# Top-k attention and an MLP on one core: last rows selected first, VectorE turning them, and another order of the first steps

## The chip, the core and the metric

The kernel runs on one core of a Trainium2 chip. The metric is the device time of one execution in microseconds (us); the median of three runs before the change is 1659.19 us (1656.96 to 1659.20). The profile is one execution of 1655.8 us from first to last instruction.

The core's engines run side by side and wait for each other by semaphores: TensorE (PE; its weight loads are PEld), VectorE (DVE), ScalarE (ACT), GpSimd (POOL), and SyncE (SP), which here only issues DMA transfers.

## What is computed

```python
# q, k, v: (8 batches, 8 heads, 576 rows, 64)
scores = q @ k.T / sqrt(64)
kth    = 32nd largest score of each row
scores = where(scores >= kth, scores, -1e9)
attn   = exp(scores - rowmax) / (rowsum + 1e-9)
x      = concat_heads(attn @ v)                  # (8, 576, 512)
xn     = (x - mean) / sqrt(var + 1e-6) * g_ln
out    = x + relu(xn @ w_ch1) @ w_ch2            # 512 -> 2048 -> 512
```

The 576 rows of a head are four whole tiles of 128 rows and 64 last rows. Heads are handled in pairs: a **unit** is one tile number of one head pair. For a whole tile it has two halves, t = 0 and 1, one for each head (128 x 576 scores each); for the last rows both heads share one half (64 + 64 rows).

## The kernel before

There are 160 units. They are processed in steps, one per unit: in step `n` VectorE selects unit `n`, while other engines work on its neighbours. Units belong to groups; from batch 2 on a batch has for each of its four head pairs one group with tiles 0, 1 and the last rows, and later one with tiles 2 and 3. A group is multiplied with the values together, one step after its last unit has been turned.

Selection of the 32nd largest score uses a split: the row's 576 scores are halved into pairs, the larger of each pair goes to `hi`, the smaller to `lo`. GpSimd makes `lo` in two passes, with integers:

```python
def halve(u):
    nc.vector.tensor_tensor(hi, a, b, ALU.max)                                  # L375
    nc.gpsimd.tensor_tensor(lo..I32, a..I32, hi..I32, ALU.subtract)             # L376
    nc.gpsimd.tensor_tensor(lo..I32, lo..I32, b..I32, ALU.add)                  # L379

def select(u, i):
    # i == 0: the 16 largest of lo, by MAX8 (L391) and match_replace (L386), appended to hi
    # i == 1, 2, 3: the 32 largest of hi, 8 at a time, MAX8 (L399) and match_replace (L386)
    #               i == 1 takes the first 8, i == 2 the next 8, i == 3 the last 16
```

After the selection ScalarE masks (L426) and exponentiates (L436) the scores into `e`. To be multiplied with the values, `e` must be turned (keys to partitions) into the tile `pt`, which has one buffer. There are two ways. TensorE transposes 128x128 pieces into PSUM and ScalarE copies them:

```python
def turn(u):
    def part(t):                    # 4 transposes (L490), then copies into pt
        for c in range(J):
            nc.tensor.transpose(ps[...], u.e[:, t, ...], ident[:])
        # last rows: two copies of 128x256 (L497); whole tile: one of 128x512 (L502)
    def last():                     # the keys left over at the end
        # last rows: two transposes (L510, L511) and two copies (L513)
        # whole tile: one transpose (L519) and one copy (L520)
    heads = () if u.moved else range(len(u.tiles))
    return [lambda t=t: part(t) for t in heads] + [last]
```

Or the unit is **moved**: VectorE turns blocks of 32x32, and two DMAs through HBM put the blocks in place. `last()` is still done by TensorE:

```python
def move(u):
    for t in range(2):
        nc.vector.transpose(blocks..., u.e[:, t, ...])          # L468, 128x512 each
    nc.sync.dma_start(hbm[:], blocks)                           # L473
    for j in range(4):
        nc.sync.dma_start(to..., hbm[:, j * 2 * P : (j + 1) * 2 * P]...)        # L476

for u in units[jobs[5 * NHP].first :]:                          # batches 2 to 7
    u.moved = not u.rest and u is not u.group.units[-1]
```

`rest` means last rows. The group's last unit is never moved.

The MLP's weights are unpacked while the first steps run. ScalarE and GpSimd split a piece (L183 to L190), VectorE shifts it (L193), GpSimd joins it (L199, L201); 32 pieces are spread over steps -1 to 15, four in the first batch, then one or two in a step:

```python
def weights(n, phase):
    if phase == 0:
        for x in batches.get(n + 1, []): x.fetch()
        for x in now[0::2]: x.split()
    elif phase == 1:
        for x in before: x.shift()
        for x in before: x.join()
        for x in now[1::2]: x.split()
```

The MLP's matmuls (`hidden` L664, `project` L680) wait in a list `todo` and are let out in small portions at eight places of each step, so that TensorE has work between the attention's parts. `share` is what a place may let out, `owed` what has been saved up:

```python
def fill(least=0):
    owed[0] = min(owed[0] + share[0], 6.0)
    while todo and ...:
        if owed[0] < todo[0][1] / 2 and least <= 0: break
        pop()

def slot(n):
    if n <= CONVERTING:                                # 17
        return max(0.0, dve_cost(n) - pe_cost(n)) / SLOTS       # SLOTS = 8
    ...                                                # later: what is left, spread evenly
                                                       # up to the next block of rows
```

The main part, cut to what is spoken of below:

```python
load(fresh[0], nc.sync, nc.scalar)
...
turn_heads(fresh[0])
scores(units[0])                     # TensorE L354, ScalarE copies L335
halve(units[0])
load_gain()
weights(-1, 0)
weights(-1, 1)
for n in range(END):
    if n in gives: give(n)           # a block of rows enters todo; the first at n = 9
    share[0] = slot(n)
    u, nxt, mk = at(n), at(n + 1), at(n - 1)
    late = at(n - 4)                 # last rows whose outputs are placed now
    for x in due(n): scores(x)       # unit n + 1 at first, n + 2 after step 17
    if u: select(u, 0)
    ...
    weights(n, 0)
    fill() ...
    if u: select(u, 1)
    if nxt: halve(nxt)
    if n in turns: turn_heads(turns[n])          # VectorE L306
    weights(n, 1)
    fill() ...
    if u: select(u, 2)
    ...
    if u: select(u, 3)
    if moved: move(ex)               # ex: the unit two steps back
    fill()
```

Of the kernel before, what the change touches and what calls it, by code (L numbers as in the profile page):

```python
# [10 lines left out]
ALU = mybir.AluOpType  # L11
FP32 = mybir.dt.float32
# [9 lines left out]
J = 4  # L22
# [7 lines left out]
def kernel(  # L30
# [41 lines left out]
    nc = tc.nc  # L72
    P = nc.NUM_PARTITIONS
# [4 lines left out]
    JP = J * P  # L78
    R = S - JP
# [131 lines left out]
    def load_gain():  # L211
        ps = turned()
        nc.tensor.transpose(ps[:, 0:NC], grow[:], ident[0:NC, 0:NC])
        nc.scalar.copy(gcol[:], ps[:, 0:NC])
# [8 lines left out]

    def weights(n, phase):

        now, before = batches.get(n, []), batches.get(n - 1, [])
        if phase == 0:
            for x in batches.get(n + 1, []):
                x.fetch()
            for x in now[0::2]:  # L230
                x.split()
        elif phase == 1:
            for x in before:
                x.shift()
            for x in before:
                x.join()
            for x in now[1::2]:
                x.split()
# [81 lines left out]
    class Group:  # L320
        def __init__(self, job, qts):
            self.job, self.qts = job, qts
            self.nq = sum(R if qt == J else P for qt in qts)
            self.units = [Unit(job, self, qt) for qt in qts]
            self.pt = self.den = None
            self.quick = False
            self.sums = None
# [35 lines left out]
    def halve(u):  # L363

        nt = len(u.tiles)  # L370
        u.lo = lopool.tile([P, 2, HALF], FP32, tag="lo", name="lo")
        u.hi = hipool.tile([P, 2, HALF + TOP_K // 2], FP32, tag="hi", name="hi")
        a, b = u.sc[:, 0:nt, 0:HALF], u.sc[:, 0:nt, HALF:S]
        lo, hi = u.lo[:, 0:nt], u.hi[:, 0:nt, 0:HALF]
        nc.vector.tensor_tensor(hi, a, b, ALU.max)  # L375
        nc.gpsimd.tensor_tensor(  # L376
            lo.bitcast(I32), a.bitcast(I32), hi.bitcast(I32), ALU.subtract
        )
        nc.gpsimd.tensor_tensor(lo.bitcast(I32), lo.bitcast(I32), b.bitcast(I32), ALU.add)  # L379
# [82 lines left out]
    def move(u):  # L462

        i0 = place_of(u)
        ni = P // 32
        blocks = u.sc[:].rearrange("p t n -> p (t n)")[:, 0 : 2 * JP]
        for t in range(2):
            nc.vector.transpose(  # L468
                blocks.rearrange("p (j t c n) -> p j t c n", j=ni, t=2, c=J)[:, :, t],
                u.e[:, t, t * R : t * R + JP].rearrange("p (c j k) -> p j c k", c=J, k=32),  # L470
            )
        hbm = hbmpool.tile([P, 2 * JP], FP32, tag="turned", name="turned")
        nc.sync.dma_start(hbm[:], blocks)  # L473
        for j in range(ni):
            to = u.group.pt[j * 32 : (j + 1) * 32, 0 : 2 * J].rearrange("k c n -> k (c n)")
            nc.sync.dma_start(  # L476
                to[:, i0 * 2 * P : (i0 + ni) * 2 * P].rearrange("k (i x) -> k i x", i=ni),
                hbm[:, j * 2 * P : (j + 1) * 2 * P].rearrange("(i k) x -> k i x", k=32),
            )
# [278 lines left out]
    EARLY = jobs[NHP].first  # L758

    for u in units[jobs[5 * NHP].first :]:  # L760
        u.moved = not u.rest and u is not u.group.units[-1]


    full = slice(0, P)
# [35 lines left out]
    def at(i):  # L800
        return units[i] if 0 <= i < N else None
# [6 lines left out]

    def due(n):

        ahead = [n + 1] if n < CONVERTING else [n + 2]
        if n == CONVERTING:
            ahead = [n + 1, n + 2]
        return [units[i] for i in ahead if i < N]
# [10 lines left out]
    def pe_cost(n):  # L825
        c = 0.0
        for x in due(n):
            c += 1.25 if x.rest else 1.5
        ex, g = after(n)
        if ex:  # L830
            c += 0.67 if ex.rest else 0.15 if ex.moved else 1.0
        if g:
            c += 0.6 + 7.8e-3 * g.nq
        return c

    def dve_cost(n):
        u, ex = at(n), after(n)[0]
        c = 4.0 if u is None else DVE_REST if u.rest else DVE_UNIT
        if n <= CONVERTING:
            c += 1.0  # L840
        c += DVE_TURN * (n in turns) + 0.85 * sum(b.n for b in gives.get(n, []))
        return c + DVE_MOVE if ex and ex.moved else c

    def give(n):
        early = not all(map(done, ready))
# [39 lines left out]
    load(fresh[1], nc.sync, nc.scalar)  # L885
    scores(units[0])
    halve(units[0])
    load_gain()
    weights(-1, 0)
    weights(-1, 1)  # L890
    for n in range(END):
        now[0] = n
        if n in gives:
            give(n)
        share[0] = slot(n)
        u, nxt, mk = at(n), at(n + 1), at(n - 1)
        ex, g = after(n)
        g = g if g and not g.quick else None
        late = at(n - 4)
        late = late if late and late.rest and late.job.b % 2 else None  # L900
        parts = turn(ex) if ex else []
        early = ex is not None and n - 1 < EARLY
        last = ex and ex is ex.group.units[-1]
        quick = ex.group if last and ex.group.quick else None

        moved = ex is not None and ex.moved
        sent, stores[:] = stores[:], []

        if ex and not early:
            weigh(ex, 0)  # L910
        for x in due(n):
            scores(x)
        if u:
            select(u, 0)
        for store in sent:
            store()
        if n == gives_first:
            for blk, i in rows_of.pop(n):
                blk.stats(i)
        if mk and mk.i >= CONVERTING:  # L920
            prepare(mk)
        if early:
            for t in range(2):
                mask(ex, t)
                weigh(ex, t)
        if not quick:
            weights(n, 0)
        fill()
        if ex and len(ex.tiles) > 1 and not early:
            weigh(ex, 1)  # L930
        fill()
        if g:
            values(g)
        if parts and not moved:
            parts[0]()
        if ex and ex.rest:
            keep_den(ex)
        if u:
            select(u, 1)
        if nxt:  # L940
            halve(nxt)
        for den in recips.pop(n, []):
            nc.vector.reciprocal(den, den)
        if n in turns:
            turn_heads(turns[n])
            later = fresh.index(turns[n]) + 1
            if later < len(fresh):
                load(fresh[later], nc.sync, nc.sync)
        if not quick:
            weights(n, 1)  # L950
        fill()
        if mk and not early:
            mask(mk, 0)
        if g:
            place(g)
        if late:
            place_rest(late.job.b, late.job.hp)
        fill(1 if g or late else 0)
        fill()
        if len(parts) > 2:  # L960
            parts[1]()
        if u:
            select(u, 2)
        for blk, i in rows_of.pop(n, []):
            blk.stats(i)
        for blk in gives.get(n - 2, []):
            blk.inverse()
        if last and ex.group.sums is not None:
            recips.setdefault(n + 1, []).append(ex.group.sums)
        last_rest = at(n - 3)  # L970
        if last_rest and last_rest.rest and last_rest.job.b % 2:
            hp = last_rest.job.hp
            den = dr[last_rest.job.b // 2][:, 2 * hp : 2 * hp + 2]
            recips.setdefault(n + 1, []).append(den)
        fill()
        if parts:
            parts[-1]()
        if mk and len(mk.tiles) > 1 and not early:
            mask(mk, 1)
        fill()  # L980
        for x in (u if n < EARLY else None, mk if n > EARLY else None):
            if x and x is units[x.job.last]:
                load_values(x.job)
        if quick:

            values(quick)
            for den in recips.pop(n + 1):
                nc.vector.reciprocal(den, den)
            place(quick)
            weights(n, 0)  # L990
            weights(n, 1)
        if u:
            select(u, 3)
            if u.i < CONVERTING:
                prepare(u)
        if moved:
            move(ex)
        for x in (g, quick):
            if x and x.job.hp == NHP - 1:
                for qt in x.qts:  # L1000
                    if qt < J:
                        arrived(n, (x.job.b, qt), xs[x.job.b, qt])
        if late and late.job.hp == NHP - 1:
            r = late.job.b // 2
            arrived(n, ("r", r), rs[r])
        fill()
# [37 lines left out]
```

## Time and profile before

| engine | instructions | what it does here |
|---|---|---|
| TensorE | 6825 | scores, turns, values, MLP |
| VectorE | 4619 | selection, turns of heads and moved units, shifts |
| ScalarE | 2607 | copies out of PSUM, mask, exponent, splits |
| GpSimd | 879 | lower halves, joins, centring of rows |

| group of instructions | count | busy us | mean ns |
|---|---|---|---|
| L680 project, 512 columns | 1152 | 548.7 | 603 |
| L664 hidden, 256 columns | 1536 | 370.3 | 386 |
| L354 scores, 288 columns | 1024 | 181.8 | 448 |
| L399 MAX8 on hi | 1152 | 499.4 | 479 |
| L386 replace on hi | 864 | 398.4 | 477 |
| L391 MAX8 on lo | 576 | 238.8 | 458 |
| L375 hi, whole tiles | 128 | 103.7 | 811 |
| L376 and L379, lo, whole tiles | 128 each | 182.3 and 181.4 | 1424 and 1417 |
| L193 shifts | 32 | 28.2 | 921 |

How to read it: a matmul in fp32 appears as two instructions, so 1152 of L680 are 576 products. Matmuls overlap in TensorE's pipeline, so that the sum of their durations is more than their busy time; what one costs is the time from its start to the next one's start. The views used are the page with its busy shares and slices, tables of windows (busy time of each engine in a stretch of time), groups of instructions by line, lists of waits (who waited for whom), and the timeline. An arrow in a wait reads "waited for".

### The profile page before, as it was taken

How to read it: one execution, taken by the hardware profiler on the slowest of the kernel's cores; microseconds unless marked ns; L12 is line 12 of the kernel's file. 1: busy time of each engine (PE TensorE's matmuls, PEld its weight loads, DVE VectorE, ACT ScalarE, POOL GpSimd, SP SyncE). 2: the span in 40 equal slices, each digit the busy share in tenths (PEclk: the TensorE clock that was granted, in tenths of full speed). 3: DMA queues.
4: the chain of work that ended last, by engine and by line, in shares of the span. 5: the costliest groups of instructions: out<-in, count | busy, mean ns of one | idle time of the engine just before them, and what ended most of it. 6: DMA issues, size and time to landing. Idle time of an engine off the chain costs nothing.

```text
span 1655.8 us, 24475 instructions
## 1 busy us (share of the span) xinstructions
PE 1559.2 (94%) x6825; PEld 918.0 (55%) x6825; DVE 1472.6 (89%) x4619; ACT 1036.8 (63%) x2607; POOL 673.9 (41%) x879
## 2 busy tenths in 40 slices
PE   2668989989899999999999999999999999999998
PEld 1336457556355475745547575755547565755564
DVE  5997999999999999999999999999999999997000
ACT  6986877667656666666656665666656665665310
POOL 5776763343443433344243433344343433342010
PEclk9879999999999999999999999999999999999999
DMA  7422332001433334333443335233443334232000
GB/s 177 111 76 88 85 67 55 22 14 23 101 107 89 96 83 126 104 92 83 116 118 98 86 90 128 91 92 87 113 118 98 86 87 117 90 92 72 32 13 13
DMA packets 301199, 142.28 MB, mean 86 GB/s; under 512 B 246276, under 2 KB 283144, under 8 KB 301064
## 3 DMA queue, kind: packets, MB, share of 16 engines
q1 hardware_dynamic: 296328, 140.13, 31.5%
q10 hardware_dynamic: 4736, 0.59, 0.3%
q8 instruction: 55, 0.90, 0.2%
q14 instruction: 80, 0.66, 0.1%
HBM read 93.46 MB, written 47.19 MB: 85 GB/s over the span
## 4 chain that ended last, share of the span: by engine, by line
PE 71%; DVE 18%; issue 4%; ACT 4%; POOL 3%; DMA 1%; ACTq 0%; POOLq 0%; DVEq 0%
PE hps L664 25%; PE ops L680 24%; PE scps L354 8%; PE av L544 7%; DVE m L399 5%; DVE hi L386 4%; DVE hi L391 3%; PE tp L490 2%; PE av L551 2%; DVE lo L386 2%; DVE hi L375 1%; DVE size L193 1%; PE tp L648 1%; ACT sc L335 1%; PE xo L583 1%
## 5 line engine op out<-in xcount | busy, mean ns | idle before, releaser
L664 PE MATMUL hps<-xT,w 128*128 128x256 f32 (+1 forms) x2048 | 551.1, 412 | 6.1 <-ACT xT L653 6.1
L680 PE MATMUL ops<-w,h 128*128 128x512 f32 x1152 | 548.7, 603 | 0.0
L399 DVE MAX8 m<-hi 128x8 f32<-128x304 f32 x1152 | 499.4, 479 | 3.3
L664 PEld LDWEIGHTS hps<-xT,w 128*128 128x128 f32 x2048 | 373.0, 192 | 122.7 <-issue 32.1
L376 POOL TENSOR_TENSOR lo<-sc,hi 128x576 int32<-128x576 int32 (+1 forms) x160 | 208.1, 1301 | 481.9 <-DVE hi L375 225.7
L386 DVE MATCH_REPLACE8 hi<-m,hi 128x304 f32<-128x304 f32 x864 | 398.4, 477 | 0.0
L680 PEld LDWEIGHTS ops<-w,h 128*128 128x128 f32 x1152 | 200.9, 192 | 186.4 <-issue 181.4
L354 PE MATMUL scps<-kT,qT 64*128 64x288 f32 (+3 forms) x1344 | 220.0, 428 | 36.9 <-DVE qT L306 27.2
L391 DVE MAX8 hi<-lo 128x8 f32<-128x288 f32 x576 | 238.8, 458 | 12.7 <-POOL lo L379 11.6
L335 ACT COPY sc<-scps 128x288 f32<-128x288 f32 x576 | 199.5, 408 | 68.4 <-PE scps L354 54.4
L426 ACT ACTIVATE e<-sc,m 128x576 f32<-128x576 f32 x288 | 224.2, 779 | 7.6 <-DVE m L399 4.3
L436 ACT ACTIVATE e<-e,bias 128x576 f32<-128x576 f32 x288 | 224.9, 781 | 0.6
L379 POOL TENSOR_TENSOR lo<-lo,sc 128x576 int32<-128x576 int32 (+1 forms) x160 | 207.0, 1294 | 12.5
L354 PEld LDWEIGHTS scps<-kT,qT 64*128 64x128 f32 (+1 forms) x1344 | 121.7, 178 | 154.0 <-issue 60.5
L675 ACT ACTIVATE h<-hps 128x512 f32<-128x512 f32 (+1 forms) x160 | 89.1, 557 | 95.2 <-PE hps L664 94.0
L544 PE MATMUL av<-pt,vb 128*64 128x256 f32 (+2 forms) x1088 | 147.2, 413 | 0.2 <-ACT pt L513 0.2
L375 DVE TENSOR_TENSOR hi<-sc 128x576 f32<-128x576 f32 (+1 forms) x160 | 119.3, 746 | 21.3 <-ACT sc L335 21.3
L386 DVE MATCH_REPLACE8 lo<-hi,lo 128x288 f32<-128x288 f32 x288 | 127.4, 457 | 0.0
L693 POOL TENSOR_TENSOR o<-o,x 128x512 f32<-128x512 f32 x32 | 42.1, 1317 | 200.1 <-ACT o L689 200.1
L556 ACT COPY oT<-av 128x256 f32<-128x256 f32 (+2 forms) x68 | 26.2, 385 | 148.6 <-PE av L551 148.6
L544 PEld LDWEIGHTS av<-pt,vb 128*64 128x64 f32 x1088 | 73.7, 142 | 77.7 <-ACT sc L335 15.9
L490 PE MATMUL tp<-ident,e 128*128 128x128 f32 x576 | 92.0, 284 | 24.7 <-ACT e L436 24.2
(70 smaller groups left out, 1277.2 us busy)
## 6 DMA issues: line engine op xcount, KB each, us to landing
turned<-sc SPq DMA_DIRECT2D x72, 512.0 KB, 2.6
pt<-turned SPq DMA_DIRECT2D x288, 128.0 KB, 2.9
vb<-in_v_dram SPq DMA_DIRECT2D x136, 128.0 KB, 2.6
raw<-in_moe_w_ch_dram SPq DMA_DIRECT2D x32, 512.0 KB, 3.9
kin<-in_k_dram SPq DMA_DIRECT2D x128, 72.0 KB, 2.5
qin<-in_q_dram SPq DMA_DIRECT2D x120, 72.0 KB, 2.5
out_dram<-o SPq DMA_DIRECT2D x32, 256.0 KB, 2.2
ends<-in_v_dram SPq DMA_DIRECT2D x136, 16.0 KB, 2.2
```

Source lines behind the costliest of these rows:

```text
L335: nc.scalar.copy(u.sc[:, t, s * HALF : (s + 1) * HALF], made[s][t][:, 0:HALF])
L354: nc.tensor.matmul(ps[i * R : i * R + ql, o : o + width], qT[r, q0 : q0 + ql], kT[r, k0 : k0 + width], start=True, stop=True,)
L376: nc.gpsimd.tensor_tensor(lo.bitcast(I32), a.bitcast(I32), hi.bitcast(I32), ALU.subtract)
L379: nc.gpsimd.tensor_tensor(lo.bitcast(I32), lo.bitcast(I32), b.bitcast(I32), ALU.add)
L386: nc.vector.match_replace(x[:, t], m[:, t, :], x[:, t], LOWEST)
L391: nc.vector.max(u.hi[:, t, o : o + 8], u.lo[:, t])
L399: nc.vector.max(m[:, t, :], u.hi[:, t])
L426: nc.scalar.activation(u.e[:, t], u.sc[:, t], AF.Prelu, bias=u.thr[:, t, 7:8], scale=-1.0, alpha=SLOPE)
L436: nc.scalar.activation(u.e[:, t], u.e[:, t], AF.Exp, bias=u.bias[:, t : t + 1], scale=-scale / SLOPE, accum_out=g.den[:, col : col + 1],)
L544: nc.tensor.matmul(av[h * D : (h + 1) * D, 0 : g.nq], vb[:, h * J + c, :], g.blocks[:, h, 0 : g.nq // 32, c, :], start=(c == 0), stop=False,)
L664: nc.tensor.matmul(ps["h"][:, o : o + N], w1[:, c, f * P : (f + 1) * P], xT[0][:, c, 0:N], start=(c == 0), stop=(c == NC - 1),)
L680: nc.tensor.matmul(ps[i][:], hT[f][:, i * P : (i + 1) * P], w2[:, f, :], start=(f == 0), stop=(f == NF - 1),)
```

## The change

In groups with last rows, these become the first unit, the whole tiles come after. With that the last rows can be moved too: VectorE turns them and the first whole tile, and the group's last unit, now a whole tile, is turned by TensorE. For the first unit VectorE makes the lower half itself. The scores of unit 1 are made before the weights' first splits. Shifts are issued ahead of the next unit's halving. The first step of the MLP lets out less. Some cost terms of the plan are adapted, and the placing of last rows' outputs is taken two units later, since they now come two units earlier.

```diff
 def weights(n, phase):
         elif phase == 1:
-            for x in before:
-                x.shift()
             for x in before:
                 x.join()
@@ Group
-            self.units = [Unit(job, self, qt) for qt in qts]
+            order = sorted(qts, key=lambda qt: qt < J)
+            self.units = [Unit(job, self, qt) for qt in order]
@@ halve
         nc.vector.tensor_tensor(hi, a, b, ALU.max)
+        if u.i == 0:
+            nc.vector.tensor_tensor(lo, a, b, ALU.min)
+            return
@@ move
+        if u.rest:
+            blocks = u.sc[:, 0, 0:JP]
+            nc.vector.transpose(
+                blocks.rearrange("p (j c n) -> p j c n", j=ni, c=J),
+                u.e[:, 0, 0:JP].rearrange("p (c j k) -> p j c k", c=J, k=32),
+            )
+            hbm = hbmpool.tile([P, 2 * JP], FP32, tag="turned", name="turned")
+            nc.sync.dma_start(hbm[:, 0:JP], blocks)
+            for j in range(ni):
+                for h in range(2):
+                    nc.sync.dma_start(
+                        u.group.blocks[j * 32 : (j + 1) * 32, h, ...],
+                        hbm[h * R : (h + 1) * R, j * P : (j + 1) * P]...,
+                    )
+            return
@@
-        u.moved = not u.rest and u is not u.group.units[-1]
+        u.moved = u is not u.group.units[-1]
@@ due
-        ahead = [n + 1] if n < CONVERTING else [n + 2]
+        ahead = [] if n == 0 else [n + 1] if n < CONVERTING else [n + 2]
@@ pe_cost, dve_cost
-            c += 0.67 if ex.rest else 0.15 if ex.moved else 1.0
+            c += 0.15 if ex.moved else 0.67 if ex.rest else 1.0
-        return c + DVE_MOVE if ex and ex.moved else c
+        return c + DVE_MOVE / (1 + ex.rest) if ex and ex.moved else c
@@ main part
     halve(units[0])
+    scores(units[1])
     load_gain()
@@
         share[0] = slot(n)
+        if n == gives_first:
+            owed[0] = 0.0
+            share[0] /= 2
-        late = at(n - 4)
+        late = at(n - 6)
@@
             select(u, 1)
+        for x in batches.get(n - 1, []):
+            x.shift()
         if nxt:
             halve(nxt)
```

More of the change, by code (lines that the diff above doesn't have):

```diff
@@ L465, in move @@
         ni = P // 32
+        if u.rest:
[9 more added lines that the diff above has]
+                    nc.sync.dma_start(
+                        u.group.blocks[j * 32 : (j + 1) * 32, h, i0 : i0 + ni // 2].rearrange(
+                            "k i c n -> k i (c n)"
+                        ),
+                        hbm[h * R : (h + 1) * R, j * P : (j + 1) * P].rearrange(
+                            "(i k) x -> k i x", k=32
+                        ),
+                    )
+            return
         blocks = u.sc[:].rearrange("p t n -> p (t n)")[:, 0 : 2 * JP]
```

## The prediction

> **What bounds the kernel now.** I read the page's busy shares first, then the table of windows, the waits window by window, and last the timeline of single stretches.
>
> ```profile
> PE 1559.2 (94%) x6825; PEld 918.0 (55%) x6825; DVE 1472.6 (89%) x4619; ACT 1036.8 (63%) x2607; POOL 673.9 (41%) x879
> ...
> PEclk9879999999999999999999999999999999999999
> ```
> TensorE and VectorE are both near full, and TensorE's clock dips in the first slices. The windows say where the rest is:
> ```profile
> 0.00:41.00 41.00, 10.81 (x39) 6.02 (x39) 23.47 (x59) 26.10 (x51) 22.50 (x29) 1.00 0.73 179
> ...
> 30.00:124.00 94.00, 56.02 (x224) 32.19 (x224) 93.86 (x307) 81.35 (x184) 72.96 (x62) 0.81 0.39 102
> 124.00:250.00 126.00, 114.47 (x547) 72.88 (x547) 111.54 (x330) 91.95 (x222) 85.33 (x87) 0.93 0.32 81
> ...
> 580.00:1490.00 910.00, 906.09 (x4026) 535.59 (x4026) 897.18 (x2818) 577.62 (x1487) 353.69 (x497) 1.00 0.36 100
> ```
> Columns: stretch, length, busy time (and count) of PE, PEld, DVE, ACT, POOL, clock, DMA. In the first 41 us no engine is full (VectorE 23.5 of 41): work waits for work. From 30 to 124 VectorE sets the pace (93.86 of 94 us busy) and TensorE idles. From 580 to 1490 TensorE idles 3.9 us of 910 and VectorE 12.8: both are full, but TensorE more so, and after VectorE's last selection (1527) TensorE works on for 128 us. Since a modelled busy share may deceive, I looked at starts in the timeline between 580 and 1490: 256-column matmuls follow each other at 216 ns, 512-column ones at 429 ns, 128-column transposes at 109 ns, nearly without exception. So there TensorE is **the bound**: from about 580 us on, work added to it lengthens the run, and relief of VectorE alone is worth at most the 3.9 us of idle.
>
> Between 124 and 580 the two alternate. The waits of TensorE and VectorE:
> ```profile
> DVE hi L391 <- POOL lo L379: 3.0, 1, 3.0
> ...
> DVE hi L375 <- ACT sc L335: 8.1, 2, 4.2
> ...
> DVE hi L375 <- ACT sc L335: 9.5, 3, 7.0
> ...
> PE tp L648 <- POOL x L619: 4.4, 1, 4.4
> ...
> PE tp L648 <- POOL r L619: 5.3, 1, 5.3
> ```
> (total, times, longest.) The first two are from 0 to 60 us: VectorE waits for GpSimd's lower halves and for the scores of the second unit. The third, 130 to 166 us, holds one wait of 7.0 us. The last two, near 340 and 453 us, are TensorE waiting for rows that depend on VectorE: there TensorE is ahead, as the timeline also shows (at units 28 to 34 scores had been copied 10 to 18 us before VectorE took them; from unit 50 on, mostly 5 to 10 us).
>
> **What the Trainium skill says.** "Perfetto Trace Analysis", Identifying the Most-Contended Engine, calls matmul busy share a poor measure of headroom because matmuls are pipelined; that is why I went to start-to-start times, which here agree with the busy share after 580 us. "GPSIMD Engine Reference", Key points, says GpSimd shares its SBUF interfaces with VectorE and contends with 2-port modes; "VectorE: DVE Perf Modes", the perf-mode tier table, gives fp32 tensor_scalar the 2x mode. The trace fits: the shift L193 (128x512) takes 392 to 430 ns alone, but 1619 to 1636 ns as the second shift beside GpSimd's lower halves. "TensorE: Matmul & The Clock Gate", Part 1, says that an idle window of about 3.4 us brings half clock; here the 4.4 us wait is followed by clock 0.50 from 340.7 to 347.5, and the 5.3 us wait by 0.50 from 453.3 to 460.1.
>
> **The change part by part.**
>
> ```profile
> L468 DVE STREAM_TRANSPOSE sc<-e 128x512 f32<-128x512 f32 x144 | 95.0, 697 | 21.4 <-ACT e L436 21.1
> L490 PE MATMUL tp<-ident,e 128*128 128x128 f32 x576 | 92.0, 284 | 24.7 <-ACT e L436 24.2 <-ACT sc L335 0.5
> L502 ACT COPY pt<-tp 128x512 f32<-128x512 f32 x112 | 65.1, 583 | 32.4 <-PE tp L490 31.8
> L497 ACT COPY pt<-tp 128x256 f32<-128x256 f32 x64 | 20.8, 379 | 25.1 <-PE tp L490 24.9
> ```
> *1. Who turns what.* It concerns batches 2 to 7, four head pairs each: 24 groups with last rows. Before, VectorE turned both whole tiles (4 of L468) and TensorE the last rows (4 big transposes); the key ends stay on TensorE for all. After, VectorE turns the last rows and the first whole tile (1 + 2 of L468) and TensorE the second whole tile (8 big transposes). VectorE saves one L468 per group: 24 x 0.70 = **16.7 us**. TensorE gets four transposes more: 24 x 4 x 0.109 = **+10.5 us**, at the start-to-start time, since 284 ns is latency. ScalarE gets 2 x 0.583 - 2 x 0.379 = 0.41 us per group, +9.8 us; at 63% busy that hides. The sync queue issues 9 transfers for the last rows instead of 5 for a tile, at 0.4 to 0.5 us each; two steps of some 9 us lie between them and their use, against 2.6 + 2.9 us to land: hidden. Since TensorE is the bound in these batches, this part costs 10.5 us, less at most 3.9.
>
> *2. Start.* Unit 0's lower half on VectorE costs one more pass of about 0.76 us but ends the path hi (12.5), two GpSimd passes (15.5), so selection begins near 13.3 instead of 15.54: 2.2 us. The scores of unit 1 now stand ahead of the weights' splits, which held ScalarE from 12.75 to 22.44, so the 4.2 us wait goes. The four first shifts took 5.2 us beside GpSimd (25.78 to 30.99); ahead of the halving they meet an idler GpSimd and are held only by the last split, near 22 us. I get halving of unit 1 near 22.5, heads turned by 24.6, and unit 1's selection near 28.9 instead of 35.2: 6.3 us. GpSimd then has its eight joins (10.5 us), which start only about 2 us earlier than before, and unit 2's lower halves behind them: VectorE will wait some 2 us for these. Net **3 to 5 us**. Shifts ahead of the halving also save about 1.2 us at each of the few later steps where two fell beside GpSimd (81, 123 us): 2 to 3 us.
>
> *3. MLP's first step.*
> ```profile
> 123.34 2.37 DVE L193 TENSOR_SCALAR size<-size 128x512 uint32<-128x512 uint32 x2
> ...
> 125.37 13.28 PE L664 MATMUL hps<-xT,w 128*128 128x256 f32 x52 [2.95 <-ACT xT L653]
> 138.58 1.24 PE L354 MATMUL scps<-kT,qT 64*128 64x288 f32 x8
> ```
> Step 9 lets out 52 matmuls in one burst, 13.3 us, and the next scores stand behind it: this is the 7.0 us wait. By the code's own terms the burst is the saved allowance 6.0 plus eight slots of (11.3 - 4.1) / 8 = 0.9, some 13 us. Without the saved part and with half a slot it is 3.6 us: two turns and about 6 hidden products, 12 matmuls. VectorE's **7 us** go; but 40 matmuls x 0.216 = 8.6 us are only put off, to step 18, before the second block. From 140 to 200 us the steps are held at about 12.5 us by a loop (scores copied, halving, GpSimd's lower halves and joins, ScalarE's splits, the next copies), which the change does not shorten.
>
> *Sum.* VectorE's time line after step 16 lies 4 + 2.5 + 7 = 13 us earlier. TensorE has the 8.6 us to make up there, but near 340 and 453 us it used to wait for VectorE, 4.4 + 5.3 us and half a clock afterwards. So the deferred work fills those waits and the 13 us survive to about unit 43. From then on TensorE is full: +10.5. Net -2.5 us; less idle, and shorter half clocks (5.1 and 4.8 us busy at half rate there), may give one or two more: 1659.2 - 4 = **1655 us**.
>
> **Rivals.** (a) *TensorE is the bound everywhere it matters*: the early gains are used up before unit 43 (DVE gives back what it gains in GpSimd waits or in the loop), and only the +10.5 shows: 1666 to 1670. For it speak the full TensorE and the queue that never empties; against it the two waits for rows. (b) *VectorE is the bound after all*, TensorE's 0.109 us hides in slack, and 16.7 + 13 us come off: about 1630. Against it: TensorE's 128 us behind VectorE's end, which no VectorE relief shortens. (c) *A new wait*: more, smaller transfers of the last rows, or lower halves asked for later by the shifts ahead of them, hold up values or selection by about 1 us per group: 1680. Against it: two steps of slack, and 1.4 us or more between the lower halves' end and their use at steps 4 and 7.
>
> **Range and chances.** The sum lies between its two large terms, +10.5 (sure in count, and in cost where TensorE is full) and -13 (each piece can fall short by half), with the clock dips worth some us either way. I take 1644 to 1667 for 8 in 10. Two per cent are 33 us: faster by that needs rival b in full, 0.02; slower needs rival c, 0.015.
>
> **What would show it.** L468 120 instead of 144; L490 672 instead of 576; L502 160 and L497 16. TensorE's busy time up by some 10 us or a little less; VectorE's in 580 to 1490 down to about 96%, with new waits for scores. Unit 1's halving at 22 to 24 us; hps in the first burst about 12; no 7 us wait near 134. The waits for x and r near 340 and 453 short or gone. The tail behind VectorE's last selection should grow. I am wrong if TensorE does not stay full from unit 43 on, if a wait on lo or on the turned last rows takes over, or if the early gain is lost in the loop.

## The result and the profile after

| | median us | lowest to highest | runs |
|---|---|---|---|
| before | 1659.2 | 1656.96 to 1659.88 | 4 |
| changed | 1652.85 | 1652.07 to 1653.84 | 4 |

The ratio is 0.9964, 95% interval 0.9947 to 0.9982. The time fell by 6.3 us; a fall of 4 had been forecast, to 1655, within 1644 to 1667. The profiled execution took 1651.7 us against 1655.8.

Line numbers moved: L193 is the same; the halving is now L377, `lo` L382 and L385, MAX8 on `hi` L405, MAX8 on `lo` L397, the big transposes L515, hidden products L689, VectorE's turn of the last rows L474 and of whole tiles L493, ScalarE's copies after the transposes L527 (whole tile) and L522 (last rows). First the page's busy shares, then the windows (stretch, length, busy time and count of PE, PEld, DVE, ACT, POOL, clock, DMA share, GB/s):

```profile
PE 1563.9 (95%) x6921; PEld 926.6 (56%) x6921; DVE 1445.2 (87%) x4596; ACT 1050.3 (64%) x2607; POOL 666.5 (40%) x877
```

```profile
30.00:124.00 94.00, 55.35 (x224) 32.41 (x224) 89.53 (x289) 82.65 (x186) 72.06 (x61) 0.66 0.39 102
124.00:250.00 126.00, 118.65 (x610) 75.76 (x611) 109.86 (x354) 98.08 (x240) 89.15 (x94) 0.96 0.34 84
...
580.00:1490.00 910.00, 906.36 (x4059) 536.58 (x4058) 877.41 (x2774) 581.08 (x1473) 347.43 (x495) 1.00 0.33 87
```

TensorE's busy time rose by 4.7 us and VectorE's fell by 27.4, yet the span fell: TensorE's idle time went from 96.6 to 87.8 us, 4.2 us of it between 124 and 250. From 580 to 1490 TensorE is as full as before (906.36 of 910), while VectorE has gone from 897 to 877.

The groups by line show the turns as forecast:

```profile
L515 PE MATMUL tp<-ident,e 128*128 128x128 f32 x672 | 105.7, 282 | 23.3 <-ACT e L442 23.2
L527 ACT COPY pt<-tp 128x512 f32<-128x512 f32 x160 | 93.3, 584 | 74.2 <-PE tp L515 73.1
L493 DVE STREAM_TRANSPOSE sc<-e 128x512 f32<-128x512 f32 x96 | 64.0, 691 | 45.4 <-ACT e L442 45.3
L474 DVE STREAM_TRANSPOSE sc<-e 128x512 f32<-128x512 f32 x24 | 16.6, 693 | 0.0
L522 ACT COPY pt<-tp 128x256 f32<-128x256 f32 x16 | 5.2, 375 | 0.7 <-PE tp L515 0.6
```

96 + 24 = 120 turns on VectorE, 672 big transposes, 160 and 16 copies. The idle time before VectorE's turns of whole tiles has doubled: 45.4 us before L493, where it was 21.4 before L468. The waits of VectorE and TensorE between 580 and 1490 say what it is (total, times, longest):

```profile
DVE sc L493 <- ACT e L442: 22.0, 19, 2.0
...
PE hps L689 <- ACT xT L678: 2.3, 2, 1.2
```

VectorE now stands 22 us at its turns until ScalarE has exponentiated; in the same stretch before the change it was 3.4 us. That is part of its saved time come back as a wait; TensorE waits 2.3 us for rows and nothing else of size. The transfers of moved units hold up little: over the whole run the waits for them rose from 2.2 to 5.0 us, nearly all on ScalarE. To follow where the time went, I read from the timelines when VectorE halves certain units, which are at the same place in both orders:

| halving of | before | changed | difference |
|---|---|---|---|
| unit 2 | 39.1 | 39.1 | 0 |
| unit 11 | 140.9 | 132.9 | -8.0 |
| unit 20 | 231.7 | 221.0 | -10.8 |
| unit 72 (batch 3) | 696.6 | 682.8 | -13.8 |
| unit 152 (batch 7) | 1441.0 | 1434.8 | -6.2 |
| end | 1655.8 | 1651.7 | -4.1 |

Nothing is won up to unit 2, then 11 us by unit 20 and 14 by unit 72; between units 72 and 152, that is in sixteen groups with last rows, 7.6 us are lost again, and 2.1 more behind unit 152.

### The profile page after: what moved, and what is told of

The parts are those of the page before. It is cut to its first block, busy times and chain, and to the rows that moved or that the text cites. A ratio compares the mean times of both kernels' runs of the same rounds, so it can differ in the third digit from the quotient of the medians.

```text
span 1651.7 us, 24795 instructions
## 1 busy us (share of the span) xinstructions
PE 1563.9 (95%) x6921; PEld 926.6 (56%) x6921; DVE 1445.2 (87%) x4596; ACT 1050.3 (64%) x2607; POOL 666.5 (40%) x877
## 4 chain that ended last, share of the span: by engine, by line
PE 67%; DVE 21%; issue 4%; POOL 3%; ACT 3%; DMA 1%; ACTq 0%; POOLq 0%; SPq 0%; DVEq 0%
PE ops L705 24%; PE hps L689 23%; PE scps L356 8%; DVE m L405 6%; PE av L569 6%; DVE hi L392 6%; DVE hi L397 3%; PE tp L515 3%; PE av L576 2%; DVE lo L392 2%; DVE hi L377 2%; POOL lo L382 1%; POOL lo L385 1%; ACT sc L337 1%; PE xo L608 1%
## 5 line engine op out<-in xcount | busy, mean ns | idle before, releaser
L689 PE MATMUL hps<-xT,w 128*128 128x256 f32 (+1 forms) x2048 | 553.3, 412 | 6.4 <-ACT xT L678 6.4
L405 DVE MAX8 m<-hi 128x8 f32<-128x304 f32 x1152 | 488.5, 461 | 3.1
L689 PEld LDWEIGHTS hps<-xT,w 128*128 128x128 f32 x2048 | 370.9, 191 | 122.6 <-issue 34.2
L382 POOL TENSOR_TENSOR lo<-sc,hi 128x576 int32<-128x576 int32 (+1 forms) x159 | 205.0, 1289 | 484.1 <-DVE hi L377 202.7
L392 DVE MATCH_REPLACE8 hi<-m,hi 128x304 f32<-128x304 f32 x864 | 390.5, 458 | 0.0
L397 DVE MAX8 hi<-lo 128x8 f32<-128x288 f32 x576 | 233.9, 443 | 12.2 <-POOL lo L385 10.9
L385 POOL TENSOR_TENSOR lo<-lo,sc 128x576 int32<-128x576 int32 (+1 forms) x159 | 204.6, 1287 | 12.5
L527 ACT COPY pt<-tp 128x512 f32<-128x512 f32 x160 | 93.3, 584 | 74.2 <-PE tp L515 73.1
L515 PEld LDWEIGHTS tp<-ident,e 128*128 128x128 f32 x672 | 85.5, 146 | 77.6 <-ACT e L442 32.8
L515 PE MATMUL tp<-ident,e 128*128 128x128 f32 x672 | 105.7, 282 | 23.3 <-ACT e L442 23.2
L377 DVE TENSOR_TENSOR hi<-sc 128x576 f32<-128x576 f32 (+1 forms) x160 | 112.3, 702 | 12.2 <-ACT sc L337 12.1
```

Of the source, the lines that this page charges most:

```text
L382: nc.gpsimd.tensor_tensor(lo.bitcast(I32), a.bitcast(I32), hi.bitcast(I32), ALU.subtract)
L392: nc.vector.match_replace(x[:, t], m[:, t, :], x[:, t], LOWEST)
L397: nc.vector.max(u.hi[:, t, o : o + 8], u.lo[:, t])
L405: nc.vector.max(m[:, t, :], u.hi[:, t])
L515: nc.tensor.transpose(ps[:, c * P : (c + 1) * P], u.e[:, t, c * P + t * R : (c + 1) * P + t * R], ident[:],)
L689: nc.tensor.matmul(ps["h"][:, o : o + N], w1[:, c, f * P : (f + 1) * P], xT[0][:, c, 0:N], start=(c == 0), stop=(c == NC - 1),)
```

## Experiments

Theory A: TensorE is the bound from batch 2 or 3 on, so turning the second whole tile on TensorE costs time, and the first steps carry the gain. Rival B: VectorE is the bound, and its relief carries it. Single executions scatter by some 2 us around their median (the profile before is of one that took 1658.3 us, where the medians before are 1659.2 to 1660.55); small differences are therefore read from the medians and from the timelines together.

**The rows alone, the steps alone.**

```diff
 # e1_rows_only: before, with
+            order = sorted(qts, key=lambda qt: qt < J)
+        u.moved = u is not u.group.units[-1]
+        late = at(n - 6)          # and the move of last rows
 # e2_steps_only: changed, with these undone
```

> The kernel before with part 1 alone (last rows first, VectorE turns them and the first whole tile; first steps as before). Theory A (TensorE is the bound from about 500 us on, and the early gain carries the result): TensorE gets 96 transposes more, so slower by 7 to 10.5 us, about 1667 us, ratio 1.004 to 1.0065. Rival B (relief of VectorE by 16.7 us is what makes the change faster): 1645 to 1655 us, ratio 0.992 to 0.998.

> The changed kernel without part 1 (old order of units, VectorE turns both whole tiles, TensorE the last rows; all of the first steps' changes kept). Theory A: the early gain of about 11 us without the later loss, 1643 to 1648 us, ratio to before 0.990 to 0.994, so faster than the changed kernel. Rival B: the first steps alone bring little, 1655 to 1660 us, ratio about 0.998 to 1.0.

Measured: the rows alone 1665.95 us, ratio 1.0039 (1.0026 to 1.0053), **slower**, by 5.7 us where 7 to 10.5 had been expected. The steps alone 1649.99 us, ratio 0.9945 (0.9933 to 0.9958). Rival B falls: the part that gives the change its name loses time, though it relieves VectorE. How much it loses on top of the steps is not settled: the changed kernel, run again, gave a median of 1652.27 us, 2.3 above the steps alone, but its ratio was 0.9945 (0.9932 to 0.9959), the same as theirs.

**More for TensorE, less for VectorE.**

```diff
 # e5_rows_on_pe: changed, with
-        u.moved = u is not u.group.units[-1]
+        u.moved = not u.rest and u is not u.group.units[-1]
 # e6_half_the_turns: before, with (second turns left out, old scores sent instead)
-        for t in range(2):
+        for t in range(1):
             nc.vector.transpose(
```

> The changed kernel, last rows still first, but they are turned by TensorE again, so that VectorE turns only the first whole tile: TensorE 96 transposes more than in the changed kernel, VectorE 24 turns of 0.70 us less. Theory A (TensorE is the bound in batches 2 to 7): slower than the changed kernel by 6 to 10.5 us, 1659 to 1663 us, ratio to before 1.000 to 1.003. Rival B (relief of VectorE pays): at or below the changed kernel, 1645 to 1653 us, ratio below 0.9965.

> The kernel before, with the second of each moved unit's two VectorE turns left out (72 of 144; old scores are sent in their place, so the output is not the reference's). VectorE is relieved of 72 x 0.69 = 50 us, TensorE's work is unchanged. Theory A: at most the idle time of TensorE from 470 to 1500 us, 5 us, can be won: 1654 to 1660 us, ratio 0.997 to 1.0. Rival B: 30 us or more, below 1630 us.

With 96 further transposes and 16.7 us less of VectorE: 1659.91 us, ratio 0.9996 (0.9988 to 1.0004), 7 us above the changed kernel. With 72 turns of 0.70 us, 50 us, left out on VectorE and TensorE unchanged: 1656.91 us, ratio 0.998 (0.997 to 0.9989), 3.6 us for 50. The window from 470 to 1500, first before, then of this kernel:

```profile
470.00:1500.00 1030.00, 1025.11 (x4512) 596.76 (x4508) 1015.28 (x3192) 655.65 (x1693) 399.02 (x562) 1.00 0.36 99
```

```profile
470.00:1500.00 1030.00, 1026.56 (x4511) 597.43 (x4509) 976.12 (x3133) 657.32 (x1694) 394.09 (x563) 1.00 0.37 100
```

VectorE goes from 1015 to 976 of 1030 us, TensorE stays full, 1025 and 1027. So time follows TensorE's work, and relief of VectorE is nearly worthless there. (The added transposes also bring added copies on ScalarE; no run separates the two, but ScalarE is busy for 64% of the changed kernel's span.) The clearest scale is the time between the halvings of units 72 and 152, with sixteen groups in between:

| kernel | big transposes, all groups | units 72 to 152, us |
|---|---|---|
| before | 576 | 744.4 |
| half of VectorE's turns | 576 | 743.2 |
| steps alone | 576 | 745.3 |
| rows alone | 672 | 752.4 |
| changed | 672 | 752.0 |
| changed, last rows on TensorE | 768 | 757.3 |

The first 64 transposes more in these groups cost 8.0 us (rows alone against before) or 6.7 us (changed against the steps alone), 0.10 to 0.125 us each, the next 64 5.3 us, 0.08 each; 0.109 was the forecast.

**MLP's first step alone, the start alone.**

```diff
 # e3_mlp_only: before, with
+        if n == gives_first:
+            owed[0] = 0.0
+            share[0] /= 2
 # e4_start_only: before, with unit 0's lower half on VectorE, scores(units[1]) early, shifts ahead
```

> The kernel before with only the smaller first step of the MLP (saved allowance dropped, half a slot). Theory A: this carries most of the early gain, VectorE 7 to 8 us earlier from unit 11 on, and the time 5 to 9 us lower, about 1652 us, ratio 0.9945 to 0.997. Rival C (the work is only put off and TensorE does it later all the same): no difference, 1659 us, ratio 0.999 to 1.001.

> The kernel before with only the start (first lower half on VectorE, second unit's scores early, shifts ahead of the halving). Theory A, as the trace after shows it: unit 1 is selected 6.5 us earlier, but all of it is lost at unit 2 where the second shift waits for GpSimd behind its joins; at most 0.5 to 3 us from faster shifts remain: 1656 to 1659 us, ratio 0.998 to 1.0. Rival D (the start carries the gain): 1652 to 1654 us, ratio below 0.997.

The first: 1656.26 us, ratio 0.9975 (0.9966 to 0.9984). Unit 11 comes 6.8 us earlier, as expected, but the end only 4.7 us: behind unit 152 this kernel takes 217.0 us where the kernel before takes 214.9. All profiled kernels here that have the smaller first step take 216.9 to 217.3, and all that have not (but for the one with half the turns) 214.8 to 215.0. So some 2 us of the put-off work seem to come back at the very end.

The second surprised me: 1653.73 us, ratio 0.9963 (0.995 to 0.9975), where 0.998 to 1.0 was expected. The two sum to 10.5 us, and the steps alone, which have both, gave 10.3.

**What in the start it is.**

```diff
 # e12_shift_only: before, with only this moved ahead of halve(nxt)
+        for x in batches.get(n - 1, []):
+            x.shift()
 # e11_start_no_shift: the rest of the start, shifts where they were
```

> The start without the shifts ahead of the halving: first lower half on VectorE and early scores alone. In the trace of the whole start unit 2 came no earlier than before, and VectorE gained at steps 6 to 8 and 13 to 19, where shifts are cheaper. Theory G (the start's gain is the shifts'): no difference, 1658 to 1661 us, ratio 0.9985 to 1.0005. Rival D (early scores carry it): 1653 to 1656 us, ratio 0.996 to 0.9975.

> The kernel before with the shifts ahead of the halving, nothing else. Theory G: this alone gives what the start gave, 1653 to 1657 us, ratio 0.996 to 0.998, with the shifts' busy time falling from 28 to 17 or 18 us. Rival D: 1658 to 1661 us.

The shifts alone: 1653.84 us, ratio 0.9961 (0.9949 to 0.9974). The rest of the start: 1658.19 us, ratio 0.9986 (0.9979 to 0.9992). The shifts alone give as much as the whole start (6.5 us each), so nearly all of its gain is the order of two VectorE instructions. The two parts do not add up: 6.5 and 2.1 us apart, 6.5 together. The group of the shifts, first before, then with only them moved (group, busy time and mean ns, idle time before):

```profile
L193 DVE TENSOR_SCALAR size<-size 128x512 uint32<-128x512 uint32 x32 | 28.2, 921 | 0.0
```

```profile
L193 DVE TENSOR_SCALAR size<-size 128x512 uint32<-128x512 uint32 x32 | 16.6, 534 | 8.4 <-POOL size L190 8.4
```

And GpSimd's two passes for the lower half in the timeline of one step, again before, then with the shifts moved (in the second kernel the line numbers are smaller by two):

```profile
154.65 1.58 POOL L376 TENSOR_TENSOR lo<-sc,hi 128x576 int32<-128x576 int32 x1
156.31 1.49 POOL L379 TENSOR_TENSOR lo<-lo,sc 128x576 int32<-128x576 int32 x1
```

```profile
153.04 1.42 POOL L374 TENSOR_TENSOR lo<-sc,hi 128x576 int32<-128x576 int32 x1
154.54 1.41 POOL L377 TENSOR_TENSOR lo<-lo,sc 128x576 int32<-128x576 int32 x1
```

Both sides were slowed where they ran beside each other. The 11.6 us of busy time on VectorE come back in part as 8.4 us of waits. But GpSimd's passes lie in the loop that sets the steps from 140 to 200 us, and each step saves 0.24 us of them: from unit 11 to unit 16 the time fell from 61.4 to 60.3 us. That is 1.1 of the 4.4 us by which this trace is shorter. From unit 2 to unit 11 it wins 2.1 us, from 16 to 20 another 1.6, which I have not traced to single instructions.

**The order in batch 1, and late shifts.**

```diff
 # e7_order_batch1: steps alone, with last rows first where job.b == 1
 # e8_late_shift: steps alone, with; e10_changed_late: changed, with
-        if u.i == 0:
+        if u.i in (0, 2):
-        for x in batches.get(n - 1, []):
+        for x in batches.get(n - 1, []) if n != 1 else []:
             select(u, 3)
+            if n == 1: shift batches[0]; weights(1, 1)
```

> The first steps' changes alone, with last rows first only in batch 1 (where nothing is moved), old order and turns in batches 2 to 7. The changed kernel's TensorE idles 5.5 us less than that with the first steps alone, 3.5 us of it between 250 and 470 us. Theory E (the new order in batch 1 brings the last rows' block earlier, so that TensorE waits less for it): 2 to 4 us below the first steps alone (1650.0), 1646 to 1648 us, ratio 0.992 to 0.9935. Rival (the lesser idle is only the other side of the added transposes): same as the first steps alone, 1649 to 1651 us, ratio 0.994 to 0.995.

> The first steps' changes alone, but in step 1 the two shifts and joins come after the selection, and unit 2's lower half is made on VectorE. In the changed kernel's trace VectorE waits 4.3 us in step 1 for the second piece, whose clamp stands behind GpSimd's eight joins, and the 6.5 us won for unit 1 are gone at unit 2. Theory A: unit 2 is selected near 40 us instead of 44, VectorE stays 3 to 4 us earlier, and the time falls by 2 to 4 us below the first steps alone, 1646 to 1648 us, ratio 0.992 to 0.9935. Rival F (another wait in the weights' chain takes it back before step 9): no change, ratio 0.994 to 0.995.

> The changed kernel itself, beside the next run on the same chip. As measured before: ratio 0.9964, about 1653 us; above the first steps alone (ratio 0.9945) by 2 to 4 us if theory A holds.

> The changed kernel with the late shifts and joins in step 1 and unit 2's lower half on VectorE. On the first steps alone this gave 1648.6 against 1650.0 us, hardly more than the scatter, and 2 us in the trace. Theory A: the same 2 us here, 1650 to 1652 us, ratio 0.9945 to 0.9955. Rival F: no difference from the changed kernel.

The order in batch 1: 1649.61 us, ratio 0.9936 (0.9924 to 0.9949), hardly apart from the steps alone; its waits for rows are 5.1 and 2.9 us against 5.3 and 3.9. It doesn't explain why the changed kernel's TensorE idles 5.5 us less. The windows from 420 to 470 show half of that, first of the steps alone, then of the changed kernel:

```profile
420.00:470.00 50.00, 43.59 (x171) 23.13 (x170) 48.52 (x148) 28.48 (x76) 20.59 (x33) 0.93 0.45 118
```

```profile
420.00:470.00 50.00, 46.34 (x185) 25.41 (x184) 47.52 (x144) 31.27 (x79) 20.32 (x33) 0.93 0.40 103
```

There, in batch 2, TensorE still had 6.4 us to spare, and with the moved rows it has 3.7; another 2.5 us less of idle time lie between 580 and 1490. At unit 72 the changed kernel is 2.7 us ahead of the steps alone. So by VectorE's halvings the first eight groups do not cost, and the later sixteen do. (These times are VectorE's. MLP work that TensorE puts off in the first groups would show only later.)

The late shift: 1648.58 us, where 1646 to 1648 had been expected, ratio 0.9933 (0.9919 to 0.9946), the **lowest median of all versions**, 4.3 us below the changed kernel's first median and 1.4 below the steps alone, which is within the scatter. In the trace the end comes 1.9 us earlier than with the steps alone. On the changed kernel itself the same edit gave 1650.39 us (ratio 0.9936, 0.9924 to 0.9949) against 1652.27 on the same chip (0.9945, 0.9932 to 0.9959): again 1.9 us, again overlapping intervals. Its timeline, VectorE around the halving of unit 2:

```profile
33.00 1.67 DVE L376 TENSOR_TENSOR hi<-sc 128x576 f32<-128x576 f32 x1
34.59 1.83 DVE L379 TENSOR_TENSOR lo<-sc 128x576 f32<-128x576 f32 x1
...
40.39 0.73 DVE L193 TENSOR_SCALAR size<-size 128x512 uint32<-128x512 uint32 x2
41.29 0.80 DVE L396 MAX8 hi<-lo 128x8 f32<-128x288 f32 x2
```

Unit 2 is halved at 33 instead of 39 us, but the two passes take 1.67 and 1.83 us beside GpSimd's joins instead of 0.75, and the selection begins at 41.3 instead of 44.0, not at 40. At unit 11, 1.7 us of this are left.

## Why the prediction was right, and where it was not

**The bound** held. TensorE full, VectorE nearly, relief of VectorE worth little: 50 us less of it gave 3.6 us, where "at most the 3.9 us of idle" had been said for the stretch up to 1490. Rival (a) is out, since VectorE is still 13.8 us ahead at unit 72, and so is rival (b), since the rows alone are slower. The wait of rival (c) did not come. "Nearly without exception" was too strong: in the records between 580 and 1490 about one step in seven behind a 512-column matmul and one in eleven behind a 256-column one was longer, mostly by some 0.1 us. What shows the bound is the runs, not these steps.

**Part 1** held in count and in price: 96 transposes, and 6.7 to 8.0 us for the 64 of units 72 to 152, where 64 x 0.109 = 7.0 was forecast. TensorE's busy time rose by 10.3 us with the rows alone and by 9.4 on top of the steps, where 10.5 was forecast. What failed is "TensorE is the bound in these batches": in the first of them it was not full yet (with the steps alone it was busy for 43.59 of 50 us between 420 and 470). Hence 5.7 us for the rows alone, and 0 to 3 on top of the steps, instead of 10.5 less 3.9.

**The start** was mis-sized, in both of its terms. Unit 1's selection was said to begin at 28.9 and does at 28.7:

```profile
28.70 0.81 DVE L397 MAX8 hi<-lo 128x8 f32<-128x288 f32 x2
...
32.63 1.36 DVE L193 TENSOR_SCALAR size<-size 128x512 uint32<-128x512 uint32 x1
...
38.32 0.82 DVE L193 TENSOR_SCALAR size<-size 128x512 uint32<-128x512 uint32 x1 [4.33 <-POOL size L190]
39.06 0.74 DVE L377 TENSOR_TENSOR hi<-sc 128x576 f32<-128x576 f32 x1
```

But I had looked for 2 us of wait on the lower halves of unit 2. The wait is one instruction earlier, at the second shift, which needs the last operation of its piece's split (a clamp on GpSimd, L190). That one stands behind GpSimd's eight joins, and these begin only 0.6 us earlier than before (27.28 instead of 27.86), not 2. Unit 1's selection was 6.5 us ahead, unit 2 is halved at 39.1 as before: "net 3 to 5 us" was zero there. The place of the shift is not to blame: in the run without shifts ahead unit 2 is halved at 32.8, but the second shift waits behind it for the same clamp until 39.1, and the selection begins at 44.1, as in the changed kernel (44.0). The other term, shifts that no longer run beside GpSimd, was put at 2 to 3 us and gave 6.5 by the medians, 4.4 in the trace. The sentence that the change does not shorten the loop from 140 to 200 us was wrong: I had counted the time of the shift, and not that of GpSimd's passes beside it. That is 1.1 us in the trace; the 2.1 us up to unit 11 are about what was forecast, and 1.6 us between units 16 and 20 had not been thought of.

**MLP's first step** went as forecast where it happens:

```profile
124.19 4.85 PE L689 MATMUL hps<-xT,w 128*128 128x256 f32 x12 [3.00 <-ACT xT L678]
128.97 1.24 PE L356 MATMUL scps<-kT,qT 64*128 64x288 f32 x8
```

The burst is 12 matmuls, and with this step alone unit 11 comes 6.8 us earlier. But in time it is worth 4.0 us, not 7: the put-off work is not wholly hidden.

**The waits for rows** did not go. Between 250 and 580, after the change:

```profile
PE tp L673 <- POOL r L644: 3.7, 1, 3.7
PE tp L673 <- POOL x L644: 3.1, 2, 2.8
```

They were 5.3 and 4.4, so 2.9 us are gone, not most. And the deferred work filled only 0.5 of these: with the steps alone, and with the MLP's first step alone, the waits are still 5.3 and 3.9. The rest came with part 1; with the rows alone they are 4.8 and 3.5. Nor did the tail behind VectorE's last selection grow (126 us, before 128), nor did VectorE come to wait for scores: its slack went into waits for ScalarE at the turns.

**The sum** was right to 2 us partly by luck. Forecast: start -6.5, MLP -7, part 1 up to +10.5. Measured as medians, each alone: start without shifts -2.1, shifts -6.5, MLP -4.0, which would be 12.6 but is 10.3 together, and part 1 0 to +3. The 6.5 us of the whole start are the forecast's number, but made up otherwise: the shifts alone give as much. Forecast was too large a gain in the first steps, 13 instead of 10.3 us, against too large a loss later.

**Open**: why part 1 costs 5.7 us alone and less on top of the steps. TensorE's account tells only how: with the rows alone 10.3 us more of busy time and 1.5 us less of idle, on top of the steps 9.4 more and 5.5 less. Why the steps leave idle time that part 1 can fill is not shown, and the difference itself lies within the intervals.

## What to carry to other kernels

Where an engine's queue is full from start to start, price work on it by its start-to-start time (here 0.109 us, and 0.08 to 0.125 was paid); find from which point on that is so before multiplying by all instances. Where two instructions on different engines lengthen each other, as the shifts and GpSimd's passes do here, place one where the other engine is waiting, and count what both lose, above all if the other one lies in the loop that sets the pace. A gain at the head of a chain is worth what the next in-order wait leaves of it: follow the queue one instruction further than the first wait that goes.

## What I had not expected of the hardware

VectorE's two-tensor passes were stretched beside GpSimd's two-tensor passes as well: in the run with late shifts 1.67 and 1.83 us instead of 0.75 for 128x576, and the joins beside them 1.67 and 1.79 instead of 1.27. In the other direction a VectorE shift of 0.8 to 1.6 us lengthened GpSimd's passes from 1.41 to 1.58 and 1.49.

A long half clock near the start cost little, if anything. The changed kernel's first profile had TensorE at half clock for 41 us, from 15.6 to 56.6. A later execution of the same kernel did not have it and took 1650.5 us against 1651.7; unit 2 was halved at 39.3 in it, against 39.1, and unit 11 at 132.0, against 132.9. The 1.2 us between the ends are no more than single executions scatter. In the first 41 us TensorE is busy for only 12.7.
